# A gated mix of recurrent attention and a GEGLU network: the last down pass over all eight banks, smaller transfers, and one store moved to another queue

## The chip, the cores and the metric

The kernel runs on one core of a Trainium2 chip. The core has a matrix engine (PE, with PEld its weight loads), a vector engine (DVE), a scalar engine (ACT), GpSimd (POOL) and a sync engine (SP) that here only issues transfers. SP, ACT and POOL each issue DMA transfers from a queue of their own, in program order. The metric is the device time of one execution in microseconds (us). The kernel before took 2201.01 us, the median of three runs (2196.97 to 2208.47).

## The reference, cut to what matters

For x of 2048 rows by 1024 columns, the kernel computes `g * a + (1 - g) * b`:

- `g = sigmoid(sum(x * gate_w))`, one number for each row.
- `b = (gelu(x @ w_gate) * (x @ w_up)) @ w_down`, with a hidden width of 3584.
- `a` is a recurrence over 64 segments of 32 rows. The 8 memory rows that stand before a segment and its 32 rows of x make 40 rows `h`. From `h` come q, k and v for 32 heads of 128, then softmax attention under a mask, then the output projection Wo. The first 8 rows of the result are the memory of the next segment, and the other 32 are the segment's output.

A segment can't begin before the memory of the one before it is there, so the 64 segments run in a row. All is in bfloat16, with sums in float32.

## The kernel before, in words

**The order of the work.** Everything is one program. A small planner (`_Prog`) takes the operations in the order in which the code names them, gives each to its engine's queue, and works out which semaphores an operation must wait for. An operation waits at the head of its queue, and what is behind it waits too. Each transfer belongs to a lane, which is a semaphore; two transfers of one lane never run together, because the second waits for the first. Data in DRAM are named by keys such as `("D", "out", T)`: two transfers that write the same key run one after the other. At the end SP waits once for every lane (L137, L152 to L153).

**The feed-forward stage.** Rows are taken in four blocks of 512 (`fb`). In a block, 28 columns of tiles `j` are each made by 16 matmuls of 128x512 (L1068), followed by a chain ACT, DVE, ACT, DVE, DVE (L1076 to L1084) that leaves `GT[j]`. The down pass follows (L1134): 28 `j`, each four matmuls for each half of the block (two of its four row tiles). In the first three blocks w_down is streamed through three buffers `wd` of four `j` each (1 MB), forwards for the first half and backwards for the second. In the last block all of w_down lies in one tile `wdF`; the pass runs over all `j` for one half in banks DN and again over all `j` for the other half in banks HB. During the second run the code puts in three of the four first projections ("fills") of segment 0, and it starts the loads of the attention weights whose memory becomes free (`begin`). `mix` scales a result by `1 - g` and stores it in `b_scr`. `do_x` transposes a tile of x; `put` stores it from ACT, both the whole tile (`xq_scr`) and the last 8 rows of its segments (`xr_scr`). `dot_x` and `gate` make `g`; four tiny stores for each block put `g` into `gt_scr`.

**The recurrent stage.** 24 rows of each segment and the 8 memory rows go through the projections in the order that `walk` fixes, eight pieces of weight for each of k, q, v, Wo in two halves `u` of 16 heads. Step names such as (q, 0, 2) are: projection, half of the segment, number in the half. The 8 rows of x that are not in the 24 come from fills, done for four segments at a time (`fill`, `fill_evac`, `fill_put`, `FILL`): two fills in segments with s mod 4 = 0 and 1, one in the others. The k and q fills go through `qk_scr` in DRAM and come back with `load_qk`. Their stores are issued by POOL (L932) on one lane, "fq".

**Weights.** Most pieces (512 KB, 128 rows of 4 KB) stay in SBUF. Fourteen slots are shared by the two halves, and each is loaded again in every segment when its last reader is done: two of k, two of q, five of v, five of Wo (pieces 0, 1, 4, 5, 6). `GROUPS` says which are loaded as one transfer; `spent` holds the pieces of a group until all are free:

```python
GROUPS = {("k", 0): 2, ("q", 0): 2, ("v", 0): 3, ("v", 3): 2, ("o", 0): 1, ("o", 1): 1, ("o", 4): 3}
```

Wo is used at (o, 0) in the pairs 0 and 4, 1 and 5, 2 and 6, 3 and 7 (L850). So 0 and 4 come free first, and the group 4, 5, 6 is issued only after the third pair. The other half is used at (o, 1) in the order 2, 3, 0, 1 and, in the next segment's head, 7, 4, 5, 6 (L867).

**The last segment and the end.** Five Wo pieces of the other half ("moved") are loaded into slots of k and q, and `load_oR` brings back what attention left for the rows that take part in the last matmuls (L1189: 256 of 128x512). `blend` (L709) mixes 16 tiles of 128 rows on DVE and stores them from ACT; the eight results of L1189 are mixed at L1197 and stored by SP (L1200). Both kinds of store write keys `("D", "out", T)`.

Of the kernel before, what the change touches and what calls it, by code (L numbers as in the profile page):

```python
# [30 lines left out]
class _Prog:  # L31
# [73 lines left out]
    def finish(self):  # L105
# [6 lines left out]
        for o in self.ops:  # L112
# [20 lines left out]
            o.clock = ck  # L133

    def emit(self, block):
        self.finish()
        by = {e: [o for o in self.ops if o.eng == e] for e in self.ENGS}  # L137
        finals = [(ln[0], ln[1]) for ln in self.lanes.values()]
# [72 lines left out]
def bass_gated_mix__memory_aug_recurrent_mem_tr__geglu_ffn__prompt_kernel(  # L211
# [34 lines left out]
    with ExitStack() as es:  # L246
# [18 lines left out]
        gt_scr = nc.dram_tensor("gt_scr", [NSEG, SEG, 1], FP32)  # L265
# [107 lines left out]
        GROUPS = {("k", 0): 2, ("q", 0): 2, ("v", 0): 3, ("v", 3): 2, ("o", 0): 1, ("o", 1): 1, ("o", 4): 3}  # L373
# [105 lines left out]
        WD = 4  # L479
# [6 lines left out]
        wd = [al(f"wd{i}", [128, WD, D]) for i in range(3)]  # L486
# [20 lines left out]
        xT = al("xT", [128, TB, 4, KC, SEG])  # L507
        assert cur[0] == edge(29)
# [3 lines left out]
        assert cur[0] == edge(43)  # L512
        osbF = [al(f"osbF{t}", [128, D], at=edge(28) + 2 * D * t) for t in range(2)]
        wdF = al("wdF", [128, NJ, D], at=edge(29))
        GT = al("GT", [128, NJ, FB])
        assert cur[0] == edge(50) and len(hosts) == 50
        for n in range(4):
            stage[f"X{n}"] = al(f"X{n}", [128, 512], at=edge(49) + 1024 * n)
        for n in range(3):
            stage[f"Y{n}"] = al(f"Y{n}", [128, 512], at=kT.off + 1024 * n)  # L520
# [24 lines left out]
        def do_x(T):  # L545
            t = px[T % NPX]
            b = T % 2 + (4, 4, 0, 4)[T // TB]
# [4 lines left out]
            def f(e):  # L552
# [10 lines left out]
            op("dve", lambda e: e.tensor_copy(to, PBV[b].rearrange("p (k i c) -> p k i c", k=KC, i=4)[:, :, :, NR:SEG]),  # L563
               rd=[BK(b)], wr=[to_r])

            def put():
                op("act", lambda e: e.dma_start(xq_scr[T, :, :, :], xo[0].rearrange("p i k c -> p i (k c)")),
                   rd=[xo[1](0, 4)], wr=[("D", "xq", T)], lane=f"xw{x2}")
                if T > 0:
                    op("act", lambda e: e.dma_start(xr_scr[T], to.rearrange("p k i c -> p (k i c)")),  # L570
                       rd=[to_r], wr=[("D", "xr", T)], lane=f"xv{x2}")
# [5 lines left out]
        def dot_x(T):  # L577
            t = px[T % NPX]
            op("pool", lambda e: e.tensor_tensor(out=gp[:, :], in0=t[:, :], in1=gwb[:, :], op=ALU.mult),
               rd=[t.r(), gwb.r()], wr=[gp.r()])  # L580
            op("dve", lambda e: e.tensor_reduce(dl[:, T:T + 1], gp[:, :], AX.X, ALU.add), rd=[gp.r()], wr=[dl.r(T, T + 1)])
# [35 lines left out]
        def load_wd(c):  # L617
            op("sp", lambda e: e.dma_start(wd[c % 3][:, :, :],
                                           B_w_down[c * WD * 128:(c + 1) * WD * 128, :].rearrange("(j p) f -> p j f", p=128)),
               wr=[wd[c % 3].r()], lane=f"wd{c % 3}")  # L620
# [4 lines left out]
        def mix(T, c0, c1, b):  # L625
            ob = (osbF if T >= NT - TB else osb)[T % 2]
# [3 lines left out]
               rd=[ob.r(c0, c1)], wr=[("D", "b", T, c0)], lane=f"bo{T % 2}{c0 // 512}")  # L630

        def gate(fb):
            c = slice(TB * fb, TB * fb + TB)
            r = lambda t: t.r(TB * fb, TB * fb + TB)
            op("act", lambda e: e.activation(gal[:, c], dl[:, c], ACTF.Tanh, scale=0.5), rd=[r(dl)], wr=[r(gal)])
            op("dve", lambda e: e.tensor_scalar(out=oml[:, c], in0=gal[:, c], scalar1=-0.5, scalar2=0.5, op0=ALU.mult, op1=ALU.add),
# [3 lines left out]
            for T in range(TB * fb, TB * fb + TB):  # L640
                op("pool", lambda e, T=T: e.dma_start(gt_scr[4 * T:4 * T + 4, :, :].rearrange("s r o -> (s r) o"), gal[:, T:T + 1]),
                   rd=[r(gal)], wr=[("D", "gt", T)], lane=f"gt{T % TB}")
# [5 lines left out]
        jF = {1: (0, 1), 6: (1, 3), 13: (3, NWD)}  # L648

        def load_wdF(c):  # L650
            op("sp", lambda e: e.dma_start(wdF[:, c * WD:(c + 1) * WD, :],
                                           B_w_down[c * WD * 128:(c + 1) * WD * 128, :].rearrange("(j p) f -> p j f", p=128)),
               wr=[wdF.r(c * WD * D, (c + 1) * WD * D)], lane=f"wd{c % 3}")
# [9 lines left out]
        op("pe", tr_mem, rd=[pm.r(), mT.r(), ident.r()], wr=[BK(6)])  # L663
        op("dve", lambda e: e.tensor_copy(mS[:, 72:80], PBV[6][:, 64:64 + NB]), rd=[BK(6)], wr=[mS.r(72, 80)])
        op("dve", lambda e: e.tensor_copy(memT[:, :], PBV[6][:, 0:64]), rd=[BK(6)], wr=[memT.r()])

# [16 lines left out]
        gR = al("gR", [128, NBK], FP32)  # L683
        assert cur[0] <= edge(19) and ab[8].off >= slots[home["v", 0, 0]].off and brb[0].off >= slots[home["v", 1, 5]].off

        def load_gates():
            for b in range(NBK):
                op("sp", lambda e, b=b: e.dma_start(gR[0:RB, b:b + 1], gt_scr[SB * b:SB * b + SB, NR:SEG, :]),
                   rd=[("D", "gt", T) for T in range(TB * b, TB * b + TB)], wr=[("gR", b)] if b else [gR.r()], lane=f"gR{b}")
# [17 lines left out]
        def blend(T):  # L707
# [4 lines left out]
            op("act", lambda e: e.dma_start(of[128 * T:128 * T + 128, :], t[:, 0:D]), rd=[t.r(0, D)], wr=[("D", "out", T)], lane=f"ol{T % 4}")  # L712
# [211 lines left out]
        def fill_put(m, u, G, st, bank=TT):  # L924
            if m == "v":
# [6 lines left out]
            op("pool", lambda e: e.dma_start(qk_scr[:, 4 * G:4 * G + 4, m4, :], st[:, :].rearrange("p (i y) -> p i y", i=4)),  # L932
               rd=[st.r()], wr=[("D", "qk", G, m, u)], lane="fq")
# [21 lines left out]
        def plan(s):  # L955
# [11 lines left out]
            if s == 0:  # L967
                on("v", 0, 0, lambda: fill0("v", 0, B2, "X3"))
# [15 lines left out]
            if s == 0:  # L984
                on("k", 1, 0, lambda: load_v(0, slice(0, 1)))
            on("k", 1, 1 if s == 0 else 4, lambda: evac(bank_of["v", 0], vA, "act"))
            if s == 0:
                on(*('k', 1, 4), lambda: scores(ua, False))
                on("k", 1, 1, lambda: fill0("k", 1, A1, "X0"))
# [249 lines left out]
```

## Time and profile before

| What | Value |
|---|---|
| Median of three runs | 2201.01 us |
| The profiled execution, its own time | 2196.2 us |
| Its span | 2194.4 us |
| Mean granted clock of PE | 0.991 |
| PE busy | 2033.8 us (93%) |
| DVE, ACT, POOL busy | 1027.1, 551.6, 443.1 us |
| SP's queue (q1): bytes | 595.52 MB |

The profile is one execution, and times count from the start of its span. The stages lie as follows in it: feed-forward up to 566 us, its last down pass to 621 us, segment 0 to about 667 us, 63 more segments to about 2131 us, the last matmuls to 2187 us. "Busy" is the time in which an engine executes. In the rows on waits the first name is who waits, then for whom, then the sum in us, how often, and the longest. In the chain, a row "DMA x<-y" is the time from the issue of a transfer to its landing; PE may work during most of it. In the table of stretches each engine has its busy time, and PEclk is the share of full speed that the clock of PE was granted.

### The profile page before, as it was taken

The page shows a single profiled execution, that of the slowest core. Times are in us where ns is not written, and L with a number is a line of the kernel's source. Part 1 is how long each engine was busy: PE and PEld are TensorE (multiplying, and loading weights), DVE is VectorE, ACT ScalarE, POOL GpSimd, SP SyncE. Part 2 cuts the span into 40 slices and gives each one's busy share as a digit, 9 for nine tenths or more (in the row PEclk, how much of TensorE's full clock was granted, in tenths as well). Part 3 has the DMA queues.
Part 4 walks back from the last instruction along what each step waited for, and adds up shares of the span by engine and source line. Part 5 has one row for each costly group of instructions (what it writes and reads, how often), then busy time and mean ns, then how long its engine had stood idle before and what let it go on. Part 6 is the DMA issues. An engine that isn't in the chain of part 4 may idle for free.

```text
span 2194.4 us, 69744 instructions
## 1 busy us (share of the span) xinstructions
PE 2033.8 (93%) x31337; PEld 972.6 (44%) x31365; DVE 1027.1 (47%) x2657; ACT 551.6 (25%) x1142; POOL 443.1 (20%) x835
## 2 busy tenths in 40 slices
PE   8999999999979899998999999999899999999878
PEld 4444444444434444444444444444444444444345
DVE  5615616436224445444454454544544545445444
ACT  3303303213112222222222222222223222222210
POOL 3000100000022222322223223222232322222110
PEclk9999999999999999999999999999999999999999
DMA  9352264364587999999899999999999999999997
GB/s 308 128 192 89 91 219 124 84 234 165 185 307 285 336 338 344 346 358 345 328 357 348 356 354 342 356 343 360 344 340 349 346 338 358 337 348 347 337 334 269
DMA packets 180106, 640.23 MB, mean 292 GB/s; under 512 B 25144, under 2 KB 74936, under 8 KB 138976
## 3 DMA queue, kind: packets, MB, share of 16 engines
q1 hardware_dynamic: 150800, 595.52, 74.3%
q0 software_dynamic: 17472, 26.41, 3.9%
q10 hardware_dynamic: 11536, 13.85, 1.8%
q8 instruction: 246, 4.03, 0.7%
q14 instruction: 52, 0.43, 0.1%
HBM read 600.00 MB, written 50.27 MB: 296 GB/s over the span
## 4 chain that ended last, share of the span: by engine, by line
PE 65%; DMA 22%; DVE 6%; ACT 3%; issue 2%; POOL 1%; ACTq 0%; SPq 0%; POOLq 0%
PE pb L834 24%; PE pb L1068 14%; DMA wall<-o_scr 9%; PE pb L1134 7%; PE pb L850 5%; PE pb L732 3%; PE pb L867 3%; PE pb L907 3%; PE pb L1189 3%; DMA o_scr<-oRc 2%; DMA sl<-v_scr 2%; DMA wd<-in_B_w_down_dram 2%; DMA qk_scr<-1S 2%; DVE oT L718 1%; DMA v_scr<-kS 1%
## 5 line engine op out<-in xcount | busy, mean ns | idle before, releaser
L834 PE MATMUL pb<-sl,hT 128*32 128x512 bf16 x12288 | 761.8, 382 | 21.4 <-DVE hT L894 8.8
L834 PEld LDWEIGHTS pb<-sl,hT 128*32 128x32 bf16 x12288 | 309.4, 97 | 328.1 <-DVE hT L894 27.6
L907 PE MATMUL pb<-sl,hR 128*32 128x512 bf16 x3072 | 213.5, 384 | 7.1 <-DMA sl<-in_A_Wk_dram 3.8
L1068 PE MATMUL pb<-xT,wg 128*128 128x512 bf16 x896 | 213.4, 381 | 5.4 <-DVE GT L1084 4.1
L1068 PE MATMUL pb<-xT,wu 128*128 128x512 bf16 x896 | 212.5, 380 | 0.0
L817 POOL COPY oRc<-oT 128x128 bf16<-128x128 bf16 x128 | 96.6, 755 | 407.6 <-DVE oT L718 407.6
L867 PE MATMUL pb<-wall,oT 128*32 128x256 bf16 x4056 | 151.0, 278 | 28.4 <-DMA wall<-o_scr 24.5
L1134 PE MATMUL pb<-wd,GT 128*128 128x512 bf16 x657 | 147.2, 382 | 7.1 <-DMA wd<-in_B_w_down_dram 6.3
L718 DVE COPY part<-pb 64x256 f32<-64x256 f32 x96 | 40.4, 421 | 237.3 <-PE pb L867 237.3
L850 PE MATMUL pb<-wall,oT 128*32 128x512 bf16 x2048 | 145.8, 381 | 5.8 <-issue 0.2
L1076 ACT ACTIVATE s<-pb 128x512 f32<-128x512 f32 x112 | 66.8, 596 | 308.8 <-PE pb L1068 269.9
L1077 DVE SCALAR_TENSOR_TENSOR tp<-s,pb 128x512 f32<-128x512 f32 x112 | 76.8, 686 | 131.9 <-ACT s L1076 131.9
L867 PEld LDWEIGHTS pb<-wall,oT 128*32 128x32 bf16 x4056 | 97.4, 97 | 87.8 <-ACT oT L715 26.3
L1068 PEld LDWEIGHTS pb<-xT,wg 128*128 128x128 bf16 x896 | 86.8, 98 | 110.8 <-DVE GT L1084 8.0
L1068 PEld LDWEIGHTS pb<-xT,wu 128*128 128x128 bf16 x896 | 87.9, 98 | 106.6 <-issue 1.6
L768 ACT ACTIVATE E<-pb 128x320 bf16<-128x320 f32 x128 | 56.0, 437 | 311.0 <-DVE pb L767 311.0
L718 DVE COPY kT<-pb 128x512 bf16<-128x512 bf16 x128 | 54.4, 425 | 159.9 <-PE pb L732 159.8
L936 POOL COPY kT<-qkr 128x128 bf16<-128x128 bf16 x128 | 37.2, 291 | 423.1 <-DVE tAB L780 222.9
L715 ACT ACTIVATE oS<-pb 128x512 bf16<-128x512 f32 x63 | 37.6, 597 | 336.0 <-PE pb L834 336.0
L780 DVE STREAM_TRANSPOSE tAB<-pAB 128x128 bf16<-128x128 bf16 x512 | 114.0, 280 | 4.4
L1081 DVE SCALAR_TENSOR_TENSOR tp<-tp,pb 128x512 f32<-128x512 f32 x112 | 77.0, 687 | 78.7 <-ACT tp L1080 78.7
L718 DVE CAST oT<-pb 128x160 bf16<-128x160 f32 x256 | 76.4, 320 | 75.6 <-PE pb L800 75.5
(113 smaller groups left out, 2208.5 us busy)
## 6 DMA issues: line engine op xcount, KB each, us to landing
sl<-v_scr SPq DMA_DIRECT2D x64, 1536.0 KB, 10.0
wall<-o_scr SPq DMA_DIRECT2D x63, 1536.0 KB, 9.2
wall<-o_scr SPq DMA_DIRECT2D x131, 512.0 KB, 5.1
sl<-k_scr SPq DMA_DIRECT2D x64, 1024.0 KB, 5.8
sl<-q_scr SPq DMA_DIRECT2D x64, 1024.0 KB, 8.3
sl<-v_scr SPq DMA_DIRECT2D x64, 1024.0 KB, 9.6
wd<-in_B_w_down_dram SPq DMA_DIRECT2D x27, 1024.0 KB, 6.7
wdF<-in_B_w_down_dram SPq DMA_DIRECT2D x7, 1024.0 KB, 8.9
```

The lines of the kernel that those rows point to most:

```text
L718: op("dve", lambda e: e.tensor_copy(o, i), rd=rd, wr=wr, after=after)
L780: return [op("dve", lambda e, c=c: e.transpose(tAB[:, c + 32 * k:c + 32 * k + 4 * w].rearrange("p (j x) -> p j x", j=4)[:, :, 0:32], pAB[: ...
L817: op("pool", lambda e: e.tensor_copy(oRc[:, :, 16 * u:16 * u + 16].rearrange("p c x -> p x c"), oT[:, :, :, 32:40].rearrange("p g j c -> p ...
L834: ins = e.matmul(PB[bk][32 * g:32 * g + 32, :], lhsT=h[:, i, :], rhs=w[:, g * 512:(g + 1) * 512], start=(n == 0), stop=(n == 7))
L850: ins = e.matmul(PB[XO][32 * g:32 * g + 32, :], lhsT=oT[:, j, x, 0:32], rhs=wall[:, na:nb + 1:nb - na, c:c + 256], start=(n == 0 and hp == 0),
L867: ins = e.matmul(PB[XO][32 * g:32 * g + 32, 256 * b:256 * b + 256], lhsT=oT[:, j, x, 0:32], rhs=w[:, c:c + 256], start=False, stop=(n % 4 ...
L907: ins = e.matmul(PB[b][32 * g:32 * g + 32, :], lhsT=h[:, k[2], :], rhs=w[:, g * 512:(g + 1) * 512], start=(n == 0), stop=(n == 7))
L1068: ins = e.matmul(PB[bk][:, 0:FB], lhsT=w[:, kc, cc:cc + 128], rhs=xT[:, :, :, kc, :].rearrange("p t i c -> p (t i) c"), start=(kc == 0), s ...
L1076: op("act", lambda e, hg=hg: e.activation(s1[:, :], hg, ACTF.Square, scale=SQ), rd=[BK(bg)], wr=[s1.r()])
L1077: op("dve", lambda e, hg=hg, t=t: e.scalar_tensor_tensor(out=t[:, :], in0=s1[:, :], scalar=1.0, in1=hg, op0=ALU.add, op1=ALU.mult), rd=[BK ...
L1081: op("dve", lambda e, hu=hu, t=t: e.scalar_tensor_tensor(out=t[:, :], in0=t[:, :], scalar=1.0, in1=hu, op0=ALU.add, op1=ALU.mult), rd=[BK( ...
L1134: ins = e.matmul(PB[bank[2 * k + hf]][:, :], lhsT=GT[:, j, tb * 128:(tb + 1) * 128], rhs=w[:, x, hf * 512:(hf + 1) * 512], start=(j == end ...
```

## The change

- **`emit`**: SP no longer waits for every lane at the end. It goes through the lanes from the latest transfer back and skips those that a wait already made implies.
- **Feed-forward.** `wd` has six buffers of two `j` instead of three of four, so loads are 512 KB. Each of the first four `do_x` has a bank of its own. The copy of the last 8 rows moves into `put`, and their store goes from ACT's queue to POOL's. `dot_x` is split in two, `gate` too; their DVE parts are emitted one or two `j` later. The transposes for the first memory (`tr_mem`) move from before the first matmul to `j` = 4. `g` is stored once, as one transfer, and read back by four transfers and four small DVE copies (`pick_gates`).
- **Last down pass.** Pieces of two `j` are taken in turn for both halves, so both sets of banks, eight in all, are open together. Each piece of `wdF` and of `GT` is free as soon as its turn is over, and `begin` is called then. `osbF` has four buffers. The fills of segment 0 come behind the pass, four in a row.
- **Segment 0.** The store, load and fill steps are set earlier or in another order. The stores of fills get a lane for each of k and q and each issuing queue.
- **Wo pieces** 4 and 5 make a group, and 6 is loaded alone.
- **`fill_put` of the second fill** (always q) is issued by ACT.
- **Last segment.** The moved pieces and the first `load_oR` are issued after the second group of v, not before it.
- **Output keys** have the half as a second part, so the two halves of a block of L1200 no longer wait for each other.

```diff
+        self.last = clocks["sp"]
...
-        finals = [(ln[0], ln[1]) for ln in self.lanes.values()]
+        finals, ck = [], dict(self.last)
+        for ln in sorted(self.lanes.values(), key=lambda ln: -ln[2].idx):
+            if ck.get(ln[0], 0) < ln[1]:
+                finals.append((ln[0], ln[1]))
+                for m, v in [*ln[2].clock.items(), (ln[0], ln[1])]:
+                    ck[m] = max(ck.get(m, 0), v)
...
-        GROUPS = {("k", 0): 2, ("q", 0): 2, ("v", 0): 3, ("v", 3): 2, ("o", 0): 1, ("o", 1): 1, ("o", 4): 3}
+        GROUPS = {("k", 0): 2, ("q", 0): 2, ("v", 0): 3, ("v", 3): 2, ("o", 0): 1, ("o", 1): 1, ("o", 4): 2, ("o", 6): 1}
...
-        WD = 4
+        WD = 2
+        NWB = 6
...
-            b = T % 2 + (4, 4, 0, 4)[T // TB]
+            b = T + 4 if T < TB else T % 2 + (4, 4, 0, 4)[T // TB]
...
-                    op("act", lambda e: e.dma_start(xr_scr[T], to.rearrange("p k i c -> p (k i c)")),
+                    op("pool", lambda e: e.dma_start(xr_scr[T], to.rearrange("p k i c -> p (k i c)")),
...
+            if fb == NFB - 1:
+                op("pool", lambda e: e.dma_start(gt_scr[:, :, :].rearrange("q r t -> (q r) t"), gal[:, :]), rd=[gal.r()], wr=[("D", "gt")], lane="gt")
...
-        jF = {1: (0, 1), 6: (1, 3), 13: (3, NWD)}
+        jF = {1: (0, 2), 6: (2, 6), 13: (6, NWD)}
...
-            op("act", lambda e: e.dma_start(of[128 * T:128 * T + 128, :], t[:, 0:D]), rd=[t.r(0, D)], wr=[("D", "out", T)], lane=f"ol{T % 4}")
+            op("act", lambda e: e.dma_start(of[128 * T:128 * T + 128, :], t[:, 0:D]), rd=[t.r(0, D)], wr=[("D", "out", T, 0), ("D", "out", T, 1)], lane=f"ol{T % 4}")
...
-        def fill_put(m, u, G, st, bank=TT):
+        def fill_put(m, u, G, st, bank=TT, by="pool"):
...
-               rd=[st.r()], wr=[("D", "qk", G, m, u)], lane="fq")
+               rd=[st.r()], wr=[("D", "qk", G, m, u)], lane=f"fq{by}{m}")
...
-                on("v", 0, 0, lambda: fill0("v", 0, B2, "X3"))
+                on("k", 0, 2, lambda: fill_put("k", 0, 1, "Y1"))
+                on("k", 1, 0, lambda: fill0("k", 1, B0, "X0"))
-                on("k", 1, 1, lambda: fill0("k", 1, A1, "X0"))
+                on("k", 1, 4, lambda: fill0("q", 1, A1, "X1"))
-                on("q", 1, 0, lambda: fill0("q", 1, B1, "X1"))
-                on("q", 1, 2, lambda: fill_put("q", 1, 0, "X1"))
-                on("q", 1, 4, lambda: load_qk(0, 1))
+                on("q", 1, 0, lambda: fill_put("q", 1, 0, "X1"))
+                on("q", 1, 0, lambda: load_qk(0, 1))
...
-                on("q", 0, 4, *late[:3])
-                on("v", 0, 4, *late[3:])
-                on("q", 1, 0, lambda: load_oR(0))
+                on("v", 0, 5, *late)
+                on("v", 0, 7, lambda: load_oR(0))
...
-                on("q", 0, 2, lambda: fill_put(*fl[1], ua, SS), **nx)
+                on("q", 0, 2, lambda: fill_put(*fl[1], ua, SS, "act"), **nx)
...
+                every = [(DN, (0, 1)), (HB, (2, 3))]
+                turns = [(c, h) for c in (0, 1) for h in (0,)] + [(c, 1) for c in (0, 1)]
+                turns += [(c, h) for c in range(2, NWD - 2) for h in (0, 1)]
+                turns += [(c, h) for h in (0, 1) for c in (NWD - 2, NWD - 1)]
+                for c, h in turns:
...
+                    if h:
+                        begin(27 + c)
+                        if c % 2 and c < NWD - 1:
+                            begin(43 + c // 2)
+                for fs in ([lambda: fill0("k", 0, A0, "Y0")], [lambda: fill0("q", 0, A1, "Y2"), lambda: fill_put("k", 0, 0, "Y0")],
+                           [lambda: fill0("v", 0, XO, "Y3"), lambda: fill_put("q", 0, 0, "Y2"), lambda: load_qk(0, 0)],
+                           [lambda: fill0("k", 0, SS, "Y1", 1, hR1), lambda: load_v(0, slice(0, 1))]):
...
-                   rd=[ob.r(lo, hi)], wr=[("D", "out", T) for T in range(4 * b, 4 * b + 4)], lane=f"or{hf}")
+                   rd=[ob.r(lo, hi)], wr=[("D", "out", T, hf) for T in range(4 * b, 4 * b + 4)], lane=f"or{hf}")
```

## The prediction

> **What bounds the kernel now.** I read the page first, then the table of stretches, then PE's waits, then the chain of each stage, then the transfers. First the page:
>
> ```profile
> PE 2033.8 (93%) x31337; PEld 972.6 (44%) x31365; DVE 1027.1 (47%) x2657; ACT 551.6 (25%) x1142; POOL 443.1 (20%) x835
> DMA  9352264364587999999899999999999999999997
> ```
>
> PE works 93% of the span, and from 670 us on the transfer engines are nearly as full. The table of stretches shows where PE is not:
>
> ```profile
> 170.00:320.00 150.00, 146.85 (x697) 66.78 (x701) 69.28 (x106) 35.92 (x61) 10.70 (x8) 1.00 0.42 133
> 625.00:670.00 45.00, 31.66 (x508) 13.49 (x500) 10.82 (x33) 8.72 (x18) 11.65 (x22) 0.85 0.67 238
> 1360.00:1460.00 100.00, 92.56 (x1928) 44.42 (x1920) 48.52 (x150) 26.90 (x60) 28.21 (x55) 1.00 0.94 350
> 2060.00:2131.00 71.00, 55.20 (x1114) 26.77 (x1108) 31.29 (x96) 15.64 (x37) 10.34 (x24) 0.91 0.94 342
> ```
>
> Segment 0 leaves PE idle for 13.3 of 45 us at a clock of 0.85, the last segments for 15.8 of 71; a usual 100 us loses 7, with PE at 93% and transfers at 94%. PE's waits name the causes:
>
> ```profile
> PE pb L891 <- DVE a_bf L882: 31.7, 33, 1.0
> PE pb L867 <- DMA wall<-o_scr: 24.5, 34, 1.6
> PE pb L834 <- DMA sl<-v_scr: 7.6, 4, 5.9
> PE pb L732 <- ACT 1S L715: 6.8, 13, 1.9
> PE pb L1134 <- DMA wd<-in_B_w_down_dram: 6.3, 6, 2.2
> PE pb L757 <- POOL kT L936: 5.1, 1, 5.1
> PE pb L732 <- ACT 0S L715: 4.2, 11, 0.6
> PE pb L1068 <- DVE GT L1084: 4.1, 3, 1.9
> ```
>
> The largest, L891, is the recurrence itself, and the change leaves it. The chain of the first stage and SP's issues late in the run:
>
> ```profile
> 117.17 8.30 DMA wd<-in_B_w_down_dram
> ...
> 153.41 9.01 DMA wd<-in_B_w_down_dram
> ```
>
> ```profile
> 2106.01 0.32 SPq L429 DMA_DIRECT2D sl<-v_scr  x1
> 2106.38 3.05 SPq L386 DMA_DIRECT2D sl<-o_scr  x5
> 2109.47 0.46 SPq L429 DMA_DIRECT2D sl<-v_scr  x1
> ...
> 2181.76 6.87 SPq L1200 DMA_DIRECT2D out_dram<-orb  x3
> 2190.42 0.54 SPq L1200 DMA_DIRECT2D out_dram<-orb  x1
> ```
>
> A load of w_down takes 8 to 9 us to land. In the last segment five Wo pieces stand before the second group of v. At the end one store is issued 2.5 us after DVE made its data (2187.12 + 0.75).
>
> **The change part by part.** The sum is made against the profiled execution, 2196.2 us (span 2194.4), which is 4.8 below the median of 2201.01.
>
> *Feed-forward, w_down.* A matmul is 0.216 us (80 in 17.27), so four `j` of a half are 3.45 us. Three buffers hold 10.4 us of work. Now the first is free at 3.45, leaving 6.9 for a landing of 8.3. With six halves it is free at 1.73, leaving 8.6 for half the bytes. A 512 KB piece every 1.73 us is 303 GB/s; the trace's 2048-byte packets took 103.6 ns in this stage, 16 engines of which carry 316, and only 8 of 14 pieces are loaded in a pass. So the 6.3 go, and with them the 1.7 lost after the longest wait, when the clock was at half for 3.41 us: -8. Bounds: 0 (pieces no earlier) and -8. `load_xT` stays 10.4 us before its use, behind one smaller load; xT landed in 7.9.
>
> *Feed-forward, ACT and DVE.* The 4.1 on GT come after runs in which ACT, DVE and PE take turns. ACT loses 14 stores of `xr`, 0.44 us median and once 2.56, the one ahead of the 1.9 wait. POOL takes them at about 0.55, behind its product of 2.13; nobody waits for them before 600 us. The first four `j` cost DVE 0.28 more each for the moved copy, 3.56 against PE's 3.45. -2, bounds -4.1 and +1. The first transposes no longer wait for DVE (0.46 + 0.38, on a path that then meets the evictions): -0.3; but the nine small transposes of `tr_mem`, 0.4 in an idle at 9.97 now, come between matmuls at `j` = 4: +0.4. Together 0, bounds 0.5 either way. Gate stores fall from 16 (0.56 each, POOL idle) to one; four copies of about 0.2 each go into a DVE idle of 3.1 at 2132: 0.
>
> *Last down pass and segment 0.* The same matmuls. Weights start to load through the whole pass, 15 MB over 48 us, so L907's waits on weights (3.8, 1.5, 0.3) should go, and osbF's 1.0. The k and q stores had one lane: the q store was issued 4.4 after the k store (643.38, 647.75), and `load_qk` only at 650.41; with two lanes about 3.5 of it goes. Against that, the four fills come after the pass: 1.84 each and 0.33 for a turn put the q fill's store at about 9 us behind the last down matmul, behind four v stores of 0.55 on POOL. With 5.9 for that store, 0.55 and 5.9 for `load_qk`, the copy to kT that scores need comes some 22 us behind the pass, while PE has 19 us of work ahead of it: a new wait near 2.5, and one near 2 on the staging tile of q. What is queued behind POOL's waiting `load_qk` is `load_v`, also late. I take 6.6 + 3.5 - 4.5, and leave 1.6 for the second half's chain being the longer one: -4. Bounds: -10 (only the qkr round trips stay of 14.1 listed waits) and +4 (none of the old waits shrinks, both new ones come).
>
> *Wo as two and one.* The trace's packets between 1000 and 1400 us: 4096 bytes 195.5 ns, 8192 bytes 339.9, 12288 bytes 492.0. Each engine moves eight rows, so the split costs 8 x (339.9 + 195.5 - 492.0) = 0.35 us of transfer time in a segment, and SP 0.32 more. Of the 24.5 us, by their place, 14 waits (10.3 us) are for piece 1, which is unchanged, and 20 (14.3 us) for the group. There PE needs piece 6 two steps, 0.5 us, after piece 4. All bytes land 0.35 later, and the last is wanted 0.5 later: 0.15 gained in 20 segments, -3; half of that for what follows in the queue: -2. The engines dip to 0.6 to 0.8 busy at 10 to 13 us behind each (o, 0), where 0.35 fits. Bounds: -7 (every group wait halved) and +22 (0.35 in 63 segments, no dip).
>
> Here the Trainium skill, "DMA: Bandwidth & Descriptors", section "Rules for kernel authors", speaks against the change: it wants at least 1 MiB in a transfer, and "Anatomy of one DMA" in the same page gives a fixed 2.0 us to each. If nothing covered that, this term would be an estimated +126 by that page. The rows show several transfers in flight with engines at 94%, which covers most of it; what stays is the third rival.
>
> *The q store on ACT.* It is issued in two of four segments. ACT spends about 0.4 in place of POOL's 0.78, after a DVE copy; what is behind it is the eviction of k, which at 1049.95 came 2.3 us after that copy, so it hides. POOL's `a_scr` store comes sooner. Waits of ACT on these stores sum to 24.9 us (16.9 + 8.0), but PE's on 0S and 1S only to 11.0, and 20 ACT waits behind those (84.9 us) are for the store of `o_scr`, which stays. -2, bounds -5 and +2 (DVE late, k's eviction late). The Trainium skill's same page, "Issuing engines are not separate DMA queues", holds that the issuer saves only its own time; by that alone this term would be -1.
>
> *Last segment.* With v first, its second group lands some 7 us earlier and the wait of 5.9 goes. But 2.5 MB of Wo in 4096-byte rows (7.8 us) then end near 2124, and `load_oR` (3.7 us in the trace) near 2127.7. With about 1 to land, the last matmuls start near 2128.7 and not 2131.3: -2.5. Bounds 0 (transfers alone decide) and -8 (the wait and the half clock of 10.24 us at 2122 both go).
>
> *End.* The last store no longer waits for the one before it; it still waits for the blend's store, as did the one before, at 2188.08. So it is issued at 2188.6 and not 2190.42, and lands 2.3 later as now: -1.8. After that landing (2192.7) SP went through 49 waits at 0.06 each from 2190.96 to 2193.9; few are left: -1.1. Together -2.9, bounds -1.5 and -3.5.
>
> Sum: -8 - 2 - 4 - 2 - 2 - 2.5 - 2.9 = -23.4, so 2172.8 for an execution like the profiled one. A median should lie a little above; half of the 4.8 (2.4) gives 2175. The rivals get the same 2.4.
>
> **The rivals.**
>
> First, *all bounds go well*: segment 0 -9, ACT -5, Wo -6, last segment -6 give 2196.2 - 10 - 26 - 2.9 + 2.4 = 2160. For it: all these waits are on the page. Against: DMA share 0.94.
>
> Second, *the four fills behind the pass take back segment 0* (+4 for -4): 2183. For it: the new waits above. Beside it, *w_down's halves land as late as before*, so that the change doesn't do this part (0 for -8): 2183 too. Against it: 8.6 us to land where 8.3 are needed, for half the bytes.
>
> Third, on the other side, *piece 6 lands late*. Place: the landing of the transfer behind the group of two. A 512 KB load of Wo takes 5.1 us to land, 1 MB of k 5.8, the 1.5 MB group 9.2. If 2 and 1 ran one behind the other, 10.9: +1.7, less the 0.5 that piece 6 is wanted later, +1.2 in 63 segments, 76 us in place of -2: 2253. It decides from 0.4 a segment, where 63 times it eats the 23.4 and the 2; at 0.58 the kernel is 11 slower. Against it: the queue moves full all the while.
>
> Fourth, *the engines are the bound*: 0.35 in each of 63 segments, +22 in place of -2: 2199, no change.
>
> **How the numbers follow.** My forecast has 0.48; the first rival 0.12, fill or halves late 0.16, the engines as bound 0.15, piece 6 late 0.09. Faster by over 0.5% (about what can be told from no change here), below 2190: 0.48 + 0.12 + 0.16 = 0.76. Within: 0.15. Slower, over 2212: 0.09. The range reaches from just below the first rival to just above the fourth, 2153 to 2200; the forecast's own is 2165 to 2186.
>
> **What would show it.** Right: no PE wait on wd; GT waits under 3; seg 0 over by about 662 in place of 667; L867's waits on wall from 24.5 to 18 to 24, DMA share 0.95; the eviction's wait on qk_scr<-1S under 5; no 5.9 on v; last store issued 0.5 after the one before; a handful of waits at the end. Wrong: periods of segments, 23.2 us in the mean from 667 to 2131, over 23.4, with L867's waits above 35; or waits on kT in segment 0 of more than 8.

## The result and the profile after

The changed kernel takes 2346.96 us, the median of four runs (2345.45 to 2351.54); the kernel before, run beside it, takes 2199.88 (2196.97 to 2208.47). The ratio is 1.067, with a 95% interval from 1.0645 to 1.0698. The profiled execution of the changed kernel has a span of 2345.9 us, 151.5 more than the one before, and a mean granted clock of 0.955 in place of 0.991.

The page after, PE's busy time and the row of the transfer engines:

```profile
PE 2089.5 (89%) x31365; PEld 993.6 (42%) x31365; DVE 1027.0 (44%) x2661; ACT 548.7 (23%) x1142; POOL 420.1 (18%) x805
DMA  9253451646768788887879788887978888787998
```

PE does the same matmuls, but is busy 55.7 us longer and has a smaller share of the span. The transfer engines were at 9 tenths nearly all through the segments, and now they swing between 7 and 9: something holds up the whole ring of work.

From the table of stretches after, the feed-forward and the usual 100 us:

```profile
170.00:320.00 150.00, 148.55 (x710) 67.69 (x709) 69.74 (x107) 36.80 (x62) 10.80 (x8) 1.00 0.41 137
...
1360.00:1460.00 100.00, 86.85 (x1710) 41.20 (x1702) 43.84 (x134) 23.68 (x53) 21.48 (x44) 0.93 0.82 304
```

The feed-forward is better (148.55 busy of 150, 146.85 before). The same 45 us around segment 0 have 35.37 busy (31.66 before; the work there runs some 10 us earlier now), and the last 71 us of segments 57.40 (55.20). The loss is in the usual 100 us, where nothing was expected to be lost: 1710 matmuls in place of 1928, clock 0.93, transfers at 82%. From (o, 0) of segment 1 to (o, 0) of segment 63, it is 1431.8 us before and 1598.4 now, 166.6 more. All other stages together are 15.1 shorter, which makes the 151.5.

PE's waits after (who waits, for whom, sum, times, longest):

```profile
PE pb L748 <- ACT 1S L731: 74.9, 15, 5.8
PE pb L748 <- ACT 0S L731: 71.9, 23, 5.2
PE pb L907 <- DVE a_bf L898: 31.8, 33, 1.0
PE pb L850 <- DMA sl<-v_scr: 4.1, 9, 1.1
PE pb L883 <- DMA wall<-o_scr: 3.6, 6, 1.5
PE pb L1082 <- DVE GT L1098: 3.5, 8, 0.9
PE pb L773 <- POOL kT L952: 3.0, 2, 2.5
```

Two rows that were 6.8 and 4.2 before make 146.8 now. The other large ones are as before or smaller, and the row on wd (6.3) is gone; small new ones are 2.8 on oR, 2.7 on hR and 1.6 on qS. ACT's waits name the transfer behind them (before: 16.9 in 13 and 8.0 in 9), and the list of issues its landing, first of before, then of after:

```profile
ACT 1S L731 <- DMA qk_scr<-1S: 97.5, 15, 7.3
ACT 0S L731 <- DMA qk_scr<-0S: 90.5, 15, 6.7
```

```profile
qk_scr<-0S POOLq DMA_DIRECT2D x15, 128.0 KB, 7.0
qk_scr<-1S POOLq DMA_DIRECT2D x15, 128.0 KB, 7.3
```

```profile
qk_scr<-0S ACTq DMA_DIRECT2D x15, 128.0 KB, 12.7
qk_scr<-1S ACTq DMA_DIRECT2D x15, 128.0 KB, 12.8
```

The same 128 KB land 5.5 to 5.7 us later when ACT issues them. The timeline of one segment after shows the whole path (start, duration, engine, line; idle time before it and what ended it in brackets), engine by engine:

```profile
1100.90 0.40 ACTq L948 DMA_DIRECT2D qk_scr<-1S  x1
...
1114.62 0.60 ACT L731 ACTIVATE 1S<-pb 128x512 bf16<-128x512 f32 x1 [7.26 <-DMA qk_scr<-1S]
...
1101.05 3.32 SPq L435 DMA_DIRECT2D sl<-v_scr  x2
...
1115.27 0.61 PE L748 MATMUL pb<-ident,1S 128*128 128x128 bf16 x4 [5.78 <-ACT 1S L731]
```

The store reads the staging tile 1S. In the same segment ACT puts the second half of k into that tile, and can't before the store has read it; PE's transposes wait for that, and all of PE's queue behind them. SP issues 2.5 MB of v 0.15 us behind the store. The stretches of the wait and of what follows it:

```profile
1109.20:1115.20 6.00, 0.28 (x20) 0.17 (x15) 0.33 (x1) 0.58 (x2) 0.29 (x1) 0.90 0.51 204
1115.20:1118.70 3.50, 3.43 (x49) 1.51 (x53) 1.08 (x3) 0.89 (x4) 0.56 (x1) 0.50 0.32 95
1118.70:1120.80 2.10, 2.10 (x32) 0.77 (x22) 1.31 (x3) 0.44 (x1) 0.41 (x2) 0.50 0.83 275
1120.90:1124.00 3.10, 3.04 (x72) 1.28 (x68) 1.71 (x8) 0.60 (x1) 0.00 (x0) 1.00 1.00 399
```

A wait costs twice: PE stands, and then its clock is granted at half for some 5.6 us of work (the transposes take 0.61 there, 0.40 at full clock). In the trace's clock records the half-clock stretches last 3.41 or 6.83 us, with few exceptions, and PE is busy for 174.4 us under them, 30.8 before. So much more work at half clock is enough for the 55.7 us that PE is busy longer. The mean time from one (o, 0) to the next shows that nearly only the segments with two fills pay: by s mod 4 it is 28.0, 29.0, 23.6, 22.4 us after, and 23.6, 23.7, 22.4, 22.7 before (without segment 0). The parts come near the 166.6: 135.8 more in the two rows and 55.7 more busy, less 20.9 on `wall`, are 170.6. It is a rough account, since these rows are of the whole run.

### The profile page after: what moved, and what is told of

The parts are those of the page before. It is cut to its first block, busy times and chain, and to the rows that moved or that the text cites. A ratio compares the mean times of both kernels' runs of the same rounds, so it can differ in the third digit from the quotient of the medians.

```text
span 2345.9 us, 69804 instructions
## 1 busy us (share of the span) xinstructions
PE 2089.5 (89%) x31365; PEld 993.6 (42%) x31365; DVE 1027.0 (44%) x2661; ACT 548.7 (23%) x1142; POOL 420.1 (18%) x805
## 4 chain that ended last, share of the span: by engine, by line
PE 61%; DMA 26%; DVE 7%; ACT 4%; issue 2%; POOL 0%; SPq 0%; ACTq 0%; POOLq 0%
PE pb L850 16%; PE pb L1082 13%; DMA qk_scr<-1S 8%; DMA qk_scr<-0S 8%; PE pb L1189 6%; PE pb L866 6%; PE pb L883 5%; PE pb L923 4%; DMA sl<-v_scr 4%; DMA wall<-o_scr 3%; PE pb L748 3%; PE pb L1234 2%; PE pb L1155 2%; DVE a_bf L898 1%; ACT vA L731 1%
## 5 line engine op out<-in xcount | busy, mean ns | idle before, releaser
L923 PE MATMUL pb<-sl,hR 128*32 128x512 bf16 x3072 | 220.4, 396 | 4.3 <-DMA hR<-xr_scr 2.7
L866 PE MATMUL pb<-wall,oT 128*32 128x512 bf16 x2048 | 188.5, 477 | 3.3
L883 PE MATMUL pb<-wall,oT 128*32 128x256 bf16 x4056 | 144.2, 277 | 7.3 <-DMA wall<-o_scr 3.6
L883 PEld LDWEIGHTS pb<-wall,oT 128*32 128x32 bf16 x4056 | 101.0, 97 | 54.5 <-ACT oT L731 26.4
L923 PEld LDWEIGHTS pb<-sl,hR 128*32 128x32 bf16 x3072 | 76.6, 101 | 77.9 <-issue 20.1
```

Source lines behind the costliest of these rows:

```text
L866: ins = e.matmul(PB[XO][32 * g:32 * g + 32, :], lhsT=oT[:, j, x, 0:32], rhs=wall[:, na:nb + 1:nb - na, c:c + 256], start=(n == 0 and hp == 0),
L883: ins = e.matmul(PB[XO][32 * g:32 * g + 32, 256 * b:256 * b + 256], lhsT=oT[:, j, x, 0:32], rhs=w[:, c:c + 256], start=False, stop=(n % 4 ...
L923: ins = e.matmul(PB[b][32 * g:32 * g + 32, :], lhsT=h[:, k[2], :], rhs=w[:, g * 512:(g + 1) * 512], start=(n == 0), stop=(n == 7))
```

## The experiments

Theory after this reading: the ACT store alone costs it, by landing late. Rivals: the Wo pieces as two and one (the prediction's third rival), and a mishap of the two together. Line numbers are those of the changed kernel.

**The store back on POOL (e1), the store alone (e2), Wo as a group of three (e3).** e1 undoes one argument; e2 makes only this edit in the kernel before (with a lane for each issuing queue); e3 is e1 with the old group.

```diff
-                on("q", 0, 2, lambda: fill_put(*fl[1], ua, SS, "act"), **nx)
+                on("q", 0, 2, lambda: fill_put(*fl[1], ua, SS), **nx)
```

```diff
-        GROUPS = {("k", 0): 2, ("q", 0): 2, ("v", 0): 3, ("v", 3): 2, ("o", 0): 1, ("o", 1): 1, ("o", 4): 2, ("o", 6): 1}
+        GROUPS = {("k", 0): 2, ("q", 0): 2, ("v", 0): 3, ("v", 3): 2, ("o", 0): 1, ("o", 1): 1, ("o", 4): 3}
```

> The changed kernel, with the q store of the second fill issued by POOL again; nothing else differs. Theory A (the ACT-issued store lands late, 12.8 us in place of about 7, and ACT's next eviction into the same tile waits for it): PE's waits on 0S and 1S fall from 146.8 us to about 10, DMA waits of ACT on qk_scr<-0S and 1S from 188 to about 25, and the time to 2347 - 140 = 2175 to 2210. Theory B (the split of Wo makes the segments slower, and the waits on 0S and 1S are only where that delay shows): time stays above 2300, and the waits move to L883.

> The kernel before, with only the q store of the second fill moved from POOL's queue to ACT's. Theory A: the store lands in about 12.8 us here too, PE waits on 0S and 1S some 140 to 150 us in all, time 2200 + 140 = 2330 to 2355. Theory B, or any theory in which the ACT store hurts only together with the other parts (the split of Wo, the new lanes): time within 1% of 2200.

> As the run with the store on POOL, and Wo pieces 4, 5 and 6 in one group of three again. If the engines' transfer time of 0.35 us a segment is what the split costs (the fourth rival), this is 15 to 22 us faster than the run with the store on POOL alone; if piece 6 lands 0.5 us after its use would allow (the third rival), 30 us or more; by the prediction's own term it is 0 to 7 us slower.

Measured beside a kernel before of 2200.33 us: e1 2181.67 (ratio 0.991, 0.9889 to 0.993), e2 2365.03 (1.0747, 1.0724 to 1.0769), e3 2182.0 (0.9925, 0.9891 to 0.9958). The store on ACT costs 165 us in both kernels (2365.03 - 2200.33, and 2346.96 - 2181.67). It is enough by itself, and without it the change gains 18.7 us. e2 lies 10 us above its range, with a landing of 12.6 and 12.8 us as expected. PE's waits on 0S and 1S in e1 are 20.8 us, above the 10 expected and the 11.0 before. Wo as two and one makes no difference that these runs can tell (e3 alone spans 20 us), though PE's waits on `wall` (L883) are 18.6 us in e1 and 23.9 in e3.

**Why it lands late: wide rows (e5).** The two forms of the store differ in their packets. The queues of the page (packets, MB, share), after and e1:

```profile
q0 software_dynamic: 16032, 23.46, 3.5%
q10 hardware_dynamic: 25216, 16.80, 2.3%
```

```profile
q0 software_dynamic: 17472, 27.40, 3.9%
q10 hardware_dynamic: 9376, 12.87, 1.7%
```

The 30 stores are 1440 packets in POOL's queue (q0), 48 for each, and 15840 in ACT's (q10), 528 for each. By their sizes in the trace POOL's are 32 of 4096 bytes and ACT's 512 of 256, each with 16 more of 4 bytes: a row of 256 bytes is a packet in ACT's queue, and POOL's packets have the bytes of 16 rows. e5 leaves the store on ACT and lays `qk_scr` out so that a row has 1024 bytes, 128 packets; a load of it then reads two rows of 256 bytes in place of one of 512.

```diff
-        qk_scr = nc.dram_tensor("qk_scr", [128, NSEG, 4, 128], BF16)
+        qk_scr = nc.dram_tensor("qk_scr", [128, NG, 4, 4, 128], BF16)
...
-            op(by, lambda e: e.dma_start(qk_scr[:, 4 * G:4 * G + 4, m4, :], st[:, :].rearrange("p (i y) -> p i y", i=4)),
+            op(by, lambda e: e.dma_start(qk_scr[:, G, m4, :, :].rearrange("p i y -> p (i y)"), st[:, :]),
```

> The changed kernel with the store still on ACT, but with the q and k scratch laid out so that a fill's four segments lie side by side: the store writes 128 rows of 1024 bytes and not 512 of 256, 8 packets for each transfer engine and not 32; the loads of it read two rows of 256 bytes for each partition where they read one of 512. Theory A1 (each engine takes turns between ACT's ring and SP's, so that a store of 32 small packets waits for some 16 large ones, 8.5 us): the packets of the store take about 2 to 3 us in place of 8.5, it lands in 6 to 7 us, PE's waits on 0S and 1S fall to below 20 us, time 2170 to 2215. Theory A2 (a store from ACT's queue is late whatever its rows, in issue or in its landing): it lands in 11 us or more and the time stays above 2300.

2200.37 us, ratio 1.0005 (0.9983 to 1.0027), landing 8.9 and 8.4 us, PE's waits on 0S and 1S 35.3. Most of the 165 goes with the number of packets, at the same bytes and the same issuer. Landing and waits stayed above what I expected.

**Three ways to change what shares the engines (e4, e8, e9), and the wide store on POOL (e6).** e4 loads all weight pieces singly, so that SP's packets have 4096 bytes; e8 stores two segments from ACT and two from POOL; e9 issues the store from SP, ahead of v in the queue of the weight loads; e6 is e1 with e5's layout, to show what the loads of short rows cost.

```diff
-        GROUPS = {("k", 0): 2, ("q", 0): 2, ("v", 0): 3, ("v", 3): 2, ("o", 0): 1, ("o", 1): 1, ("o", 4): 2, ("o", 6): 1}
+        GROUPS = {(m, i): 1 for m in PAIRS for i in PAIRS[m]}
```

```diff
+            if by == "act":
+                for x, e_ in enumerate(("act", "pool")):
+                    op(e_, lambda e, x=x: e.dma_start(qk_scr[:, 4 * G + 2 * x:4 * G + 2 * x + 2, m4, :], st[:, 256 * x:256 * x + 256].rearrange("p (i y) -> p i y", i=2)),
...
```

```diff
-                on("q", 0, 2, lambda: fill_put(*fl[1], ua, SS, "act"), **nx)
+                on("q", 0, 2, lambda: fill_put(*fl[1], ua, SS, "sp"), **nx)
```

> The changed kernel with its q store on ACT, and every weight piece loaded by a transfer of its own, so that SP's queue holds packets of 4096 bytes (about 190 ns) in place of 8192 and 12288 (385 ns in the mean beside the store). Nothing of the store changes. Turn-taking (A1): 16.6 turns of SP's ring for each engine, now of 0.19 us, make the store's packets 8.5 us -> about 3.8, its landing 12.8 -> about 8, PE's waits on 0S and 1S from 146.8 to 20 to 50; the smaller packets cost the loads themselves about 0.04 us for each of some 8 x 9 packets fewer a segment and engine, 2 to 3 us a segment, so the time stays near 2320 to 2380 whatever the store does. If the store is slow for its 256-byte rows or for its queue alone, it still lands in 12 us or more.

> The changed kernel, with the q store of the second fill cut in two: two of the four segments are stored by ACT (256 packets of 256 bytes), two by POOL. Turn-taking by packets: ACT's half has 16 packets for an engine, 8 turns, 4.3 us in place of 8.5, and lands in about 8.5 us; PE's waits on 0S and 1S near those of the wide rows on ACT, 25 to 45 us in all, time 2185 to 2210. If 256-byte rows are what is slow whatever their number, or the ACT queue has a fixed delay of 12 us, it stays at 12 us and above 2300.

> The changed kernel, with the q store of the second fill issued by SP, in the queue that holds the weight loads. Turn-taking: in the ring of the loads there is nobody to take turns with, so the 512 packets run in a row (32 x 18 ns = 0.6 us on an engine), and the store lands when the loads ahead of it are through, 5 to 9 us; PE's waits on 0S and 1S 10 to 40 us. SP waits for DVE's copy with the v loads behind it, which may cost up to 1 us in two of four segments. Time 2180 to 2225. If 256-byte rows are slow by themselves, it lands in 12 us or more.

> The run with the wide rows, with the store on POOL: it separates what the 256-byte rows of the loads cost in the wide-row run from what ACT's queue still costs there. If ACT's 8.4 to 8.9 us of landing are the rest, this is as fast as the run with the store on POOL and narrow rows, 2175 to 2188; if the loads of two short rows are, it stays at 2195 to 2205.

Beside a kernel before of 2199.83: e4 2284.97 (two runs; 1.037, 1.0303 to 1.0436), e8 2272.94 (1.0312, 1.0266 to 1.0359), e9 2178.1 (0.988, 0.9835 to 0.9924), e6 2177.98 (0.9884, 0.9836 to 0.9933). e9 settles one point: the same 512 packets land in 6.6 us when they stand in SP's queue ahead of v, so small packets are not slow by themselves. e6 came out as expected, so the loads of short rows cost nothing that shows, and what e5 lost beside it (22 us) is the store in ACT's queue. The stores of e4 and ACT's half in e8 landed at 10.6 to 11.4, well above my numbers, which went in proportion to bytes and packets; e8's time missed its range too, and e9's lies 2 us below its own. e4's lies far below its range, so the single loads did not cost the 2 to 3 us a segment that I had put. What I had overlooked came out of the next run.

**One step earlier (e10), and both cures (e11, e6's layout with e9's issuer).**

```diff
-                on("q", 0, 2, lambda: fill_put(*fl[1], ua, SS, "act"), **nx)
+                on("q", 0, 1, lambda: fill_put(*fl[1], ua, SS, "act"), **nx)
```

> The changed kernel with the second fill's turn, copy and ACT store set one step earlier in the code, at (q, 0, 1) in place of (q, 0, 2): in front of the last four Wo pieces and one step of q, which take PE about 1.3 us, so the store should be issued 1.3 to 1.5 us earlier. Theory (a landing of 12.7 us against a fixed moment at which the eviction of k needs the staging tile): the landing stays at 12 to 13 us, the eviction waits 1.4 us less in each of 30 segments, PE's waits on 0S and 1S fall from 146.8 to 95 to 115 us, and the time from 2347 to 2290 to 2315 us. Rival (the small packets slow all transfers of the segment, and the wait on the tile is only where it shows): the same bytes and packets cost the same, waits stay above 130 us, time 2330 to 2350 us. Second rival (the landing is set by when the weight loads thin out, not by the issue): the landing grows by as much as the issue is earlier, to 14 us and more, and nothing is gained.

> The changed kernel with the q store issued by SP, and qk_scr laid out so that a store is 128 rows of 1024 bytes. If the two cures add up: landing under 6.6 us, PE's waits on 0S and 1S under 10 us, time 2170 to 2178 us. If what is left of these waits is no longer the landing: waits 10 to 14 us and 2176 to 2184 us, the same as with either cure alone.

e10 took 2281.39 us, 1.032 (1.0256 to 1.0383), beside a kernel before of 2205.4. It missed all three expectations on the landing, which fell to half, and the time lies below the first one's range. Issues and ACT's waits of e10:

```profile
qk_scr<-0S ACTq DMA_DIRECT2D x15, 128.0 KB, 6.6
qk_scr<-1S ACTq DMA_DIRECT2D x15, 128.0 KB, 6.0
```

```profile
ACT 1S L731 <- DMA qk_scr<-1S: 34.9, 6, 7.6
ACT 0S L731 <- DMA qk_scr<-0S: 20.5, 3, 7.9
```

The store is issued mostly 1.83 us ahead of v now, in place of 0.15 to 0.75. In 21 of 30 segments its last packet starts 4.9 to 8.8 us after the issue, and in most of them 400 to 490 of its 512 packets run in one single microsecond, before v's packets come. In the other nine the last starts at 11.8 to 15.4, and these alone give the rows above. So the same store of 512 packets is fast or slow, and the fast ones run for the most part before v's packets come. (The time fell by less than the landing, it seems because the turn, the step that readies the store's data, comes too soon behind its own eviction now. PE waits 3.23 us for it at 762.40, 1 to 3 us in most segments, and 88.2 on 0S and 1S in all.) e11 took 2179.5 us, 0.9869 (0.9815 to 0.9923), landing 6.4 and 6.1, waits 11.1: no better than either cure alone.

**Turn by turn.** I then counted packets in the trace. The trace does not say which engine moved a packet, so numbers for each engine are all packets divided by 16. Between first and last packet of the store, SP's large packets for each of the 16 engines, medians: after 16.6, e8 15.5, e5 8.4, e4 37.3. The store has 32, 16, 8 and 32 packets for each engine. Behind it come, of v, 8 packets of 12288 bytes and 8 of 8192 for each engine (40 of 4096 in e4). The smaller of the two numbers is 16, 16, 8 and 32, near the counts but for e4's, which is 5 higher: it looks as if an engine that has both queues moves one packet of ACT's for one of SP's, whatever their sizes. In the changed kernel the second to fourth microsecond of the store have 35, 30 and 32 of its packets beside 31, 32 and 33 of SP's (means of 28 stores), in e4 85, 92 and 92 beside 79, 90 and 93. The first microsecond is not of that kind: it has 160 of the store's beside 31 in the changed kernel. That was read off afterwards, so one more run was made for it: rows of 512 bytes, 16 packets for each engine.

```diff
+        qk_scr = nc.dram_tensor("qk_scr", [128, NG, 2, 4, 2, 128], BF16)
...
+            op(by, lambda e: e.dma_start(qk_scr[:, G, :, m4, :, :].rearrange("p h i y -> p h (i y)"), st[:, :].rearrange("p (h z) -> p h z", h=2)),
```

> The changed kernel with the ACT store as 256 rows of 512 bytes (16 packets for each of the 16 engines) in place of 512 rows of 256 bytes; qk_scr is laid out for it, and its loads read two rows of 256 bytes. Theory by turns (while both queues have packets, an engine moves one of ACT's for one of SP's, whatever their sizes; behind the store's issue come 2.5 MB of v, 8 packets of 12288 bytes and 8 of 8192 for each engine): the 16 of the store need all 16 turns, so 15 to 16.5 large packets for each engine between its first and last, 6 to 7.5 us from first to last, landing 10 to 11.5 us, PE's waits on 0S and 1S 70 to 100 us, time 2255 to 2290 us. Rival by size (only packets of less than 512 bytes are slow): landing 8.5 us at most, waits 35 us at most, time 2205 us at most. Rival in proportion to the number of packets, between 128 of them (8.4 large packets for each engine, landing 8.65) and 512 (16.6 and 12.75): 11 large packets, landing 10.0, time about 2250 us.

```profile
qk_scr<-0S ACTq DMA_DIRECT2D x15, 128.0 KB, 11.3
qk_scr<-1S ACTq DMA_DIRECT2D x15, 128.0 KB, 11.8
```

16.06 large packets for each engine, 7.2 us from first to last, PE's waits 105.4 and 2292.85 us, 1.0387 (1.0332 to 1.0442), beside a kernel before of 2204.8. The count and the duration are those of the turns. One of the two landings, the waits and the time lie just above their ranges. The rival by size falls: 512 bytes cure nothing; the one in proportion falls too. In the table "turns" is the smaller of the store's and v's packets for each engine:

| Kernel | Store | Turns | Large packets counted | Landing, us | PE's waits on 0S, 1S | Median, us |
|---|---|---|---|---|---|---|
| after | ACT, 512 x 256 B | 16 | 16.6 | 12.7, 12.8 | 146.8 | 2346.96 |
| e12 | ACT, 256 x 512 B | 16 | 16.1 | 11.3, 11.8 | 105.4 | 2292.85 |
| e8 | ACT, 256 x 256 B, and POOL | 16 | 15.5 | 10.6, 11.4 | 91.3 | 2272.94 |
| e4 | ACT, 512 x 256 B, v in 4096 B | 32 | 37.3 | 10.8, 11.3 | 99.2 | 2284.97 |
| e5 | ACT, 128 x 1024 B | 8 | 8.4 | 8.9, 8.4 | 35.3 | 2200.37 |
| e1 | POOL, 32 x 4096 B | 2 | not counted | 7.0, 7.1 | 20.8 | 2181.67 |
| e9 | SP, ahead of v | none | none | 6.6, 6.6 | 12.5 | 2178.1 |

Not tried: a staging tile of its own for this store, and the lanes of k and q stores by themselves.

## Why the prediction was wrong

It said 2175 and faster; it is 2347 and slower. The step that failed is **the q store on ACT**: -2, with bounds of -5 and +2. It measured +165. The bounds were made of ACT's issue time, of a late DVE and of k's eviction; the landing stands nowhere in the term, so it was taken to stay at the 7 us of POOL's store. It was 12.7. Nothing in the trace of before said that it would stay, since ACT issues no transfer in the segments there; this should have been bounded by the far rows.

Two were at hand. ACT's waits on these stores were 24.9 us in 22 of 30 segments: the store had hardly any slack, so most of a later landing would be paid. The prediction quotes that row and reads it as cover because only 11.0 of it reached PE. And ACT's stores of `b_scr` in the same trace land 128 KB in 1.7 us where the engines are quiet and in 4.9 while weights load, 3.2 later. Taken as the upper bound, 3.2 us in 30 segments are an estimated 96 of loss, and the range would have reached far past no change; none of the rivals was this one. It would still have been short of 165: both landings lie under POOL's 7 us, and a row of `b_scr` has 1024 bytes, so these rows did not foretell the place beside v.

The Trainium skill's page "DMA: Bandwidth & Descriptors", section "Issuing engines are not separate DMA queues", holds that only the issuer's own time is saved, which the prediction made -1 for this term. Its other half, that all transfers interleave on the same engines, agrees with the counts above, but here the place in the interleaving was worth 165 us (e2) and -3.6 (e9 against e1, within what the runs scatter). The Trainium skill's section "Queues, rings and completion order", on the same page, says that an engine goes round between its queues by packets, with some 9 to 17 descriptors typical of a packet; here the counts show the profile's packets, a row each, in turn one for one (16.06 to 16 in e12), and the measurement decides. The Trainium skill's "Specifications" on that page ask for 512 bytes in a transfer for full rate; e12 has them and is 88 us slower than before all the same.

The other terms, by the borders of the stages in the traces of before, after and e1:

- *Feed-forward, w_down, ACT and DVE* (-8 and -2): right in sum. The last down pass begins at 555.62 in place of 566.13 (553.36 in e1): -10.5 to -12.8. In e2, whose feed-forward is the old one, it begins at 562.81, so some 3 of that is scatter between executions. The wait on wd is gone; that on GT is smaller only by 0.6 (3.5, eight short ones), so little of the -2 came from there.
- *Last down pass and segment 0* (-4): right. From the pass to (o, 0) of segment 1 e1 needs 112.4 us, before 116.95: -4.6. Of the two new waits, the one on kT came as 3.0, in place of the old 5.1, and the one on q's staging as 1.6 to 2.5.
- *Wo as two and one* (-2, bounds -7 and +22): the medians of e1 and e3 differ by 0.3, less than they scatter, so a term of 2 us can't be told. Waits on `wall` of 18.6 are in the 18 to 24 foretold (e3 23.9). The third and the fourth rival did not happen. The +126 that the prediction estimated by the Trainium skill for small transfers did not either; "Anatomy of one DMA" gives its 2.0 us for transfers that GpSimd issues, and SP issues these.
- *Last segment* (-2.5): right. From (o, 0) of segment 63 to the last matmuls 13.9 in e1, 16.4 before; the wait of 5.9 on v is gone.
- *End* (-2.9): right. From the end of the last matmul to the end of the span 4.3 after, 7.3 before. Of SP's 49 closing waits before, 21 stood behind the last landing (2192.7), not all 49 as the prediction reads it; after, none does. The last two stores are issued in one run of 1.18 us at 2342.53, 0.12 after DVE is done with the last result.

Without the ACT store the terms make -21.4, and e1 measured -18.7 (2200.33 to 2181.67). The agreement is in part luck. In the profiled executions e1's span is only 12.2 shorter than before's: the stages named above give 22 to 23, but the 62 segments between them take 1442.1 us in e1 and 1431.8 before, with 9.8 more in PE's waits on 0S and 1S. e9 takes 1425.9 and e6 1436.3, and what sets this is open.

Several of the signs named beforehand failed. The one that points at the cause is "the eviction's wait on qk_scr<-1S under 5", with 97.5. Periods of segments over 23.4 came too (25.8 in the mean), but by the stores, not by L867's waits, which fell to 3.6, it seems because PE's long stops gave Wo time to land; the transfer engines' share was 0.82 in the usual 100 us, not 0.95, and GT's waits 3.5, not under 3. The sign "seg 0 over by about 662 in place of 667" does not fit the prediction's own terms, which make -14 by then; (o, 0) of segment 1 came 10.4 earlier after and 17.3 in e1.

Five versions beat both kernels, by 18 to 26 us against the kernel before, and can't be told apart: POOL's store (e1 2181.67, e3 2182.0), POOL's with wide rows (e6 2177.98), SP's (e9 2178.1), SP's with wide rows (e11 2179.5).

## What to carry to other kernels

Before a transfer is moved to another queue, look at what its landing releases and whether anything already waits for it: a wait in the list, even a short one that is hidden, means that a later landing can be paid nearly in full. Here 5.7 us later in 30 segments cost 165 us (the changed kernel against e1), and 1.6 later cost 19 (e5 against e1). Then count its packets and the large ones that another queue issues within a few microseconds: in these runs it landed after about as many of these as it had packets on an engine, or after all of them where they were fewer. So it wants few packets, or a place ahead of the large load in that load's own queue. A stop of PE of some 5 us cost nearly 2 us more by the clock behind it (55.7 us over 30 stores).

## What the runs showed of the hardware that was not expected

- The same 128 KB store landed in 7.0 us from POOL, 12.7 from ACT and 6.6 from SP, while its issue took 0.77, 0.37 to 0.41 and 0.37 us. POOL's queue carried it in 32 packets of 4096 bytes, ACT's in 512 of 256, rows as the access pattern has them.
- In the changed kernel and in e4, from the second to the fourth microsecond of the store, ACT's packets and SP's went at nearly the same rate, one for one; in the changed kernel that is 256 bytes (18 ns) against 8192 or 12288 (385 ns in the mean). In a gap between loads the same packets ran at up to 490 in a microsecond.
- The first packet came 3.5 to 3.8 us after ACT's issue (medians) in all variants beside the load of v. It was 3.5 for v from SP as well, so this is not ACT's alone. Its cause stays open, as does what sets the nine late stores of e10 apart from the 21 early ones.
